# Moving transposes, casts and cluster steps between the first units of a clustered attention and SwiGLU kernel

## The chip, the cores and the metric

The program runs on one core of a Trainium2 chip (trn2). The metric is the device time of one execution in microseconds (us), lower is better; it is quoted as the median of repeated runs. The engines are called as the profile calls them: PE is TensorE's matmul pipe and PEld its weight loads, DVE is VectorE, ACT is ScalarE, POOL is GpSimd, SP is SyncE, which here only starts DMAs.

## The reference

Inputs are q, k and v (4 batches, 8 heads, 768 positions, 64 wide), 16 centroids per head, and the weights of one gated feed-forward layer (512 to 1536 and back to 512).

Each q row and each k row is assigned to the nearest centroid (argmax of the cosine). A q row attends only to the k rows of its own cluster:

```
mask = q_assign[:, :, :, None] == k_assign[:, :, None, :]
scores = where(mask, scale * q @ k.T, -1e9)
attn = softmax(scores);  x = attn @ v        (heads side by side: 3072 rows x 512)
xn = x / sqrt(mean(x*x) + 1e-6) * rms_g
out = (silu(xn @ w_gate) * (xn @ w_val)) @ w_out
```

## The kernel before, in words

**Tiling.** A *unit* is one batch and one half of its 768 query rows, so there are eight units (L47), two for each batch. A unit has 8 heads and each head has three score steps, so 24 *gaps*, counted here from 0 to 23: gap 3h+i is the step (u, h, i) of the code. In each gap `scores` (L298) makes two products of 128 keys by 384 queries on PE, into one of two PSUM buffers, and ACT takes their exponential (L312). In the second gap of a head (i = 1) `pv` (L316) multiplies the probabilities of the head before with its values: 18 matmuls into an accumulator of which there is one, shared by two heads. After the second head of a pair DVE divides by the row sum (L331, L333), and only then can the next pair's first `pv` begin.

**Cluster mask.** q and k are extended from 64 to 80 rows: the 16 rows behind hold a one-hot code of the row's cluster. The one-hot product adds a large constant exactly where the clusters agree, and the exponential's bias takes it off again. There are two ways to make the code. For unit 0's eight heads (groups 0 and 1; a *group* is four heads of a batch) `pair_clusters` (L285) treats two heads at once and `under` (L290) puts the code in place with DVE transposes. For later groups `cluster_steps` (L249) does four heads at once, for q (m = 0) and for k (m = 1): eight small products on PE (L235), a DVE transpose (L238), a maximum (L243), a comparison (L247) and a transpose back (L265); then `place` (L271) writes the code with 16 DMAs that POOL issues, the eight of q first, then the eight of k.

**Preparing a head.** `trans` (L199) transposes q or k on PE in float32 into a PSUM tile (three buffers, the tag "gen", shared with every other small product), and ACT or DVE copies it to `qkT`. `cast` (L213) brings it to bfloat16 in `qext` or `kext`, two casts of 64 x 384 for each of q and k. `vcast` (L222) does v on POOL.

**The order of the work** is written by hand: every engine does its instructions in the order in which the program emits them. Unit 0 has a table `first` (L575) that hangs work behind the gaps; gaps without an entry get `more` (L522), one warm-up matmul that keeps PE busy. `head(n)` (L534) puts k and half of q of head n in place with two `under`; `odd(n)` (L570) puts the other half of q. `late` (L574) are the transposes of group 2, with their copies on DVE. `second_batch` (L527) starts the loads of the second batch on SP, behind a tiny DMA that waits for the last division. Unit 1 runs the table `hooks` and a list of pairs (cost, work) that `attention` (L586) deals out evenly over the gaps: after gap `at` it emits as long as the cost handed out is at most total x (at + 1 - skip) / (gaps - skip). That list holds feed-forward work of unit 0 (`gv`, L376: the gate and value products, with DVE steps L393 and L397), and `prep` (L613): the casts `c` and cluster steps `a` of group 2, then transposes, casts and cluster steps of group 3. In (1, 0, 1) stands `rms(0)` (L353), the normalization of unit 0, and behind it on POOL a copy of one number, `idle` (L615), which waits for the result of `rms(0)`. From unit 2 on, the list starts with the last eight `gv` of the unit before last, then `rms(u - 1)`, the nine parts of the output product `out_mm` (L401, parts of 4 matmuls) mixed with the first transposes `xtrans` (L365), then 16 `gv` mixed with the next group's preparation. Units 2 and 3 use groups 2 and 3: group 3 is needed from gap 12 of unit 2.

**At the start**, five warm-up matmuls (`WARM`, L53) run on a memset piece of `kext[3]` (L110, L111, DVE) before the first transposes; another `busy(1)` stands at L487.

Of the kernel before, what the change touches and what calls it, by code (L numbers as in the profile page):

```python
# [10 lines left out]
BF16 = mybir.dt.bfloat16  # L11
# [11 lines left out]
def kernel(  # L23
# [12 lines left out]
    nc = tc.nc  # L36
    B, H, S, D = q.shape
# [3 lines left out]
    P = 128  # L41
# [3 lines left out]
    HG = 4  # L45
# [4 lines left out]
    FC = DF // P  # L50
    scale = 1.0 / (D ** 0.5)
    KR = D + NC
    WARM = 5  # L53
    CUT = CC + 2 * FC - 8
    LEAD = 7
    NQ, NV = 6, 8
# [3 lines left out]
    const = pool("const", 1)  # L60
# [15 lines left out]
    def src(a, n):  # L76
        b, h = divmod(n, H)
        return a[b, h].rearrange("(p t) d -> p t d", t=ST)
# [6 lines left out]
    def load_qk(n):  # L85
        if n < B * H:
            load(n, 0)
            load(n, 1)

    def load_v(n, vq=None):  # L90
        if n >= B * H:
            return
        stagedv[n] = stage.tile([P, ST, D], F32, tag="vs", name="vs", bufs=NV)
        (vq or nc.sync).dma_start(out=stagedv[n], in_=src(v, n))
# [12 lines left out]

    qext = [const.tile([P, HG, S], BF16, name=f"qext{i}") for i in range(4)]
    kext = [const.tile([P, HG, S], BF16, name=f"kext{i}") for i in range(4)]
    warm = kext[3][:, 0, :512]  # L110
    nc.vector.memset(warm, 1.0)  # L111

    def busy(n, first=True):
        to = ps_a.tile([P, 512], F32, tag="acc", name="warm") if first else \
            ps_g.tile([P, 512], F32, tag="gen", name="warm")
        for i in range(n):
            nc.tensor.matmul(to, lhsT=warm[:, :P], rhs=warm, start=True, stop=True)

    busy(WARM)


    def rsqrt(ms, n):
        half = small.tile([P, HT], I32, tag="half", name="half")[:, :n]
        nc.vector.tensor_scalar(half, ms.bitcast(I32), 1, None, op0=ALU.logical_shift_right)
        yi = small.tile([P, HT], I32, tag="yi", name="yi")[:, :n]
        nc.vector.tensor_scalar(yi, half, -1.0, float(0x5F3759DF), op0=ALU.mult, op1=ALU.add)
        y = yi.bitcast(F32)
        for i in range(3):
            a = small.tile([P, HT], F32, tag="na", name="na")[:, :n]
            nc.vector.scalar_tensor_tensor(a, y, -0.5, y, op0=ALU.mult, op1=ALU.mult)  # L130
            a2 = small.tile([P, HT], F32, tag="nb", name="nb")[:, :n]
            nc.vector.tensor_mul(a2, a, ms)
            y2 = small.tile([P, HT], F32, tag="ny", name="ny")[:, :n]
            nc.vector.scalar_tensor_tensor(y2, a2, 1.5, y, op0=ALU.add, op1=ALU.mult)
            y = y2
        return y
# [76 lines left out]
    def cast(on, g, h, part, es=(0, 1)):  # L213
        for e in es:
            to = (kext if part else qext)[g % 4][:D, h, e * UQ:(e + 1) * UQ]
            of = qkT[g, h // 2][e * D:(e + 1) * D, h % 2, part]
            if on is nc.scalar:
                nc.scalar.copy(to, of)
            else:
                on.tensor_copy(to, of)  # L220

    def vcast(n):  # L222
        nc.gpsimd.tensor_copy(vbf[n // HG % 4][:, n % HG, :, :D], stagedv[n])  # L223
# [117 lines left out]
    def squares(u, t, last):  # L341
        if (t, last) == (0, False):
            sq[u] = small.tile([P, 2, HT], F32, tag="ss", name="ss")
            xn[u] = xp.tile([P, HT, DM], BF16, tag="xn", name="xn")
        c = slice(DM - 2 * D, DM) if last else slice(0, DM - 2 * D)
        to = sq[u][:, int(last), t:t + 1]
        if u == 0:
            nc.vector.scalar_tensor_tensor(xn[u][:, t, c], xs[u][:, t, c], 1.0 / DM, xs[u][:, t, c], op0=ALU.mult,
                                           op1=ALU.mult, accum_out=to)
        else:  # L350
            nc.scalar.activation(xn[u][:, t, c], xs[u][:, t, c], ACT.Square, scale=DM ** -0.5, accum_out=to)

    def rms(u):  # L353
        x, nt = xs[u], UNITS[u][2]
        for t in range(nt):
            squares(u, t, True)
        ms = small.tile([P, HT], F32, tag="ms", name="ms")
        nc.vector.scalar_tensor_tensor(ms[:, :nt], sq[u][:, 0, :nt], 1e-6, sq[u][:, 1, :nt], op0=ALU.add, op1=ALU.add)
        y = rsqrt(ms[:, :nt], nt)
        for t in range(nt):  # L360
            nc.vector.tensor_scalar_mul(xn[u][:, t], x[:, t], y[:, t:t + 1])
# [59 lines left out]
    def group_work(g):  # L421

        t, c = [], []
        for h in range(HG):
            n = g * HG + h
            t += [(0.3, lambda h=h: trans(g, h, 0)), (0.3, lambda h=h: trans(g, h, 1))]

            def casts(h=h, n=n):
                cast(nc.gpsimd, g, h, 0)
                vcast(n)  # L430
                load_qk(n + NQ)
                load_v(n + NV)
                cast(nc.vector, g, h, 1, (0,))
            c += [(0.0, casts), (0.0, lambda h=h: cast(nc.vector, g, h, 1, (1,)))]
        a = []
        for m in range(2):
            a += [(0.0 if i else 0.7, f) for i, f in enumerate(cluster_steps(g, m))]
        a.append((0.0, lambda: [place(nc.gpsimd, g, m) for m in range(2)]))
        return t, c, a
# [5 lines left out]
    def spread(a, b):  # L445

        if not a:
            return list(b)
        w, n = [], 0
        for i, x in enumerate(a):  # L450
            w.append(x)
            while n < len(b) * (i + 1) // len(a):
                w.append(b[n])
                n += 1
        return w

    def ffn_work(u):
        n = UNITS[u][2] / HT
        w = [(0.18 * n, lambda c=c: xtrans(u, c)) for c in range(CC)]
        for f in range(FC):  # L460
            for val in (False, True):
                w.append((0.64 * n, lambda f=f, val=val: gv(u, f, val)))
        return w

    def out_work(u):
        return [(0.86, lambda t=t, p=p: out_mm(u, t, p)) for t in range(UNITS[u][2]) for p in range(3)]

    def border(o, ffn):

        return o[:-3] + ffn[:2] + o[-3:-2] + ffn[2:3] + o[-2:-1] + ffn[3:4] + o[-1:]  # L470
# [6 lines left out]
    def casts(on, n, *what):  # L477
        for m, e in what:
            cast(on, n // HG, n % HG, m, (e,))

    K0, K1, Q0, Q1 = (1, 0), (1, 1), (0, 0), (0, 1)
    pool_ = nc.gpsimd
# [1 line left out]
    trans(0, 0, 0)  # L484
    centroids_t()
    trans(0, 1, 1)
    busy(1)  # L487
    trans(0, 1, 0)
    pair_clusters(0, ps_s.tile([P, UQ], F32, tag="s", name="sc"))
    casts(pool_, 0, K0, Q0, K1)  # L490
# [31 lines left out]
    def more():  # L522
        busy(1, False)
# [3 lines left out]
    def second_batch():  # L527
        nc.sync.dma_start(out=hold, in_=invs[0].rearrange("p a t -> p (a t)"))
        for n in range(H + HG, H + NQ):
            load_qk(n)  # L530
        for n in range(H, H + NV):
            load_v(n)

    def head(n):  # L534
        under(n, 1)
        under(n, 0, 0, 1)
# [33 lines left out]
    def odd(n):  # L570
        under(n, 0, 1, 2)

    early = [lambda h=h, m=m: trans(1, h, m) for h in (2, 3) for m in (1, 0)]
    late = [lambda h=h, m=m: trans(2, h, m, nc.vector) for h in range(HG) for m in (1, 0)]  # L574
    first = {1: gap1, 2: early[0], 3: early[1], 4: lambda: (early[2](), early[3]()), 5: gap5,  # L575
             7: lambda: (more(), head(4)), 8: lambda: (more(), head(5)), 9: gap9,
             10: lambda: (more(), head(6)), 11: lambda: (more(), head(7)),
             14: lambda: (more(), odd(0), second_batch())}
    first.update({15 + i: f for i, f in enumerate(late)})
    first[16] = lambda: (late[1](), odd(1))  # L580
    first[18] = lambda: (late[3](), odd(2))


    due = []
# [22 lines left out]
    for u in range(1, NU):  # L607
        ffn, o, g = ffn_work(u - 1), out_work(u - 2) if u > 1 else [], u + 2
        if u == 1:
            t, c, a = group_work(2)  # L610
            t3, c3, a3 = group_work(3)
            n = 4
            prep = c + a + [x for h in range(HG) for x in t3[max(2 * h, n):2 * h + 2] + c3[2 * h:2 * h + 2]] + a3  # L613
            idle = const.tile([P, 1], BF16)
            hooks = {(1, 0, 1): lambda: (rms(0), nc.gpsimd.tensor_copy(idle, xn[0][:, HT - 1, DM - 1:]))}  # L615
            hooks.update({(1, *divmod(2 + i, HT)): t3[i][1] if i < n else more for i in range(LEAD - 2)})
            hooks.update({(1, h - 1, 0): lambda h=h: odd(h) for h in range(HT, H)})
            attention([(1, h) for h in range(H)], border(o, ffn) + spread(ffn[CC:CUT], prep), LEAD, hooks)
        else:
            fill = ffn_work(u - 2)[CUT:] + [(0.0, lambda u=u: rms(u - 1))] + border(o, ffn)  # L620
            attention([(u, h) for h in range(H)], fill + spread(ffn[CC:CUT], group(g) if g < NG else []), 1)
    pv(NU - 1, H - 1)
    for _, f in ffn_work(NU - 2)[CUT:]:
# [34 lines left out]
```

## Time and profile before

| what | value |
|---|---|
| median of 8 runs | 359.9 us (357.74 to 360.5) |
| the profiled execution's own time | 357.74 us |
| its span in the trace | 355.9 us |
| PE busy | 340.2 us (96%) |
| DVE busy | 232.3 us (65%) |
| ACT busy | 261.7 us (74%) |
| POOL busy | 112.7 us (32%) |
| unit 0: first and last score step | 11.60 and 36.87 us |
| unit 1: first and last score step | 37.42 and 72.25 us |
| unit 2: first and last score step | 73.24 and 113.76 us |
| unit 3: first score step | 114.89 us |

The profiled execution is the fastest of the eight. The spans of the first three units differ because they hold different work: unit 0 has no feed-forward work, unit 1 has two groups to prepare.

How to read the lines: a timeline line gives the start (us), the busy time (us), the engine, the kernel's line, the operation, output <- inputs with the shape, the number of instructions merged, and in brackets how long the engine had sat idle before and whose end released it. In a table by stretches each engine has its busy us and, in parentheses, its number of instructions.

### The profile page before, as it was taken

How to read it: one execution, taken by the hardware profiler on the slowest of the kernel's cores; microseconds unless marked ns; L12 is line 12 of the kernel's file. 1: busy time of each engine (PE TensorE's matmuls, PEld its weight loads, DVE VectorE, ACT ScalarE, POOL GpSimd, SP SyncE). 2: the span in 40 equal slices, each digit the busy share in tenths (PEclk: the TensorE clock that was granted, in tenths of full speed). 3: DMA queues.
4: the chain of work that ended last, by engine and by line, in shares of the span. 5: the costliest groups of instructions: out<-in, count | busy, mean ns of one | idle time of the engine just before them, and what ended most of it. 6: DMA issues, size and time to landing. Idle time of an engine off the chain costs nothing.

```text
span 355.9 us, 7996 instructions
## 1 busy us (share of the span) xinstructions
PE 340.2 (96%) x3028; PEld 207.8 (58%) x3028; DVE 232.3 (65%) x567; ACT 261.7 (74%) x458; POOL 112.7 (32%) x233
## 2 busy tenths in 40 slices
PE   8997898999999999999999999999999999999995
PEld 4545654555675656655575656755566656655552
DVE  4999889986368754786367864687446654674430
ACT  5996966887797868887698877978778877853431
POOL 4999064981133603353041801435000000000000
PEclk9999999999999999999999999999999999999999
DMA  7999997261162013600130001000100011001002
GB/s 268 345 235 212 264 267 246 62 189 40 59 192 80 22 59 104 194 13 14 65 113 2 21 34 61 0 6 20 59 31 0 3 44 47 3 0 67 23 2 89
DMA packets 27158, 31.62 MB, mean 89 GB/s; under 512 B 4464, under 2 KB 24176, under 8 KB 27120
## 3 DMA queue, kind: packets, MB, share of 16 engines
q1 hardware_dynamic: 17808, 24.69, 20.9%
q0 software_dynamic: 8880, 5.91, 9.7%
q8 instruction: 24, 0.39, 0.4%
q10 hardware_dynamic: 432, 0.52, 0.4%
q14 instruction: 14, 0.11, 0.1%
HBM read 28.35 MB, written 6.29 MB: 97 GB/s over the span
## 4 chain that ended last, share of the span: by engine, by line
PE 77%; POOL 7%; ACT 4%; DMA 4%; DVE 4%; issue 2%; SPq 0%; ACTq 0%; POOLq 0%; DVEq 0%
PE o L406 17%; PE val L384 15%; PE gate L384 15%; PE s L308 14%; PE acc L326 8%; PE tq L205 4%; PE sc L235 2%; ACT pT L312 2%; DMA qk<-in_q_dram 2%; POOL qext L220 2%; POOL qext L276 2%; PE tx L371 1%; POOL kext L220 1%; POOL kext L276 1%; POOL vbf L223 1%
## 5 line engine op out<-in xcount | busy, mean ns | idle before, releaser
L312 ACT ACTIVATE pT<-s,off 128x768 bf16<-128x768 f32 x192 | 171.1, 905 | 39.1 <-PE s L308 38.5
L308 PE MATMUL s<-qext,kext 80*128 80x384 bf16 x384 | 93.6, 325 | 3.1 <-ACT pT L312 2.3
L384 PE MATMUL val<-xnT,wv 128*128 128x384 bf16 x384 | 78.1, 326 | 1.8 <-DVE th L393 0.8
L384 PE MATMUL gate<-xnT,wg 128*128 128x384 bf16 x384 | 78.3, 325 | 0.4 <-DVE th L393 0.4
L393 DVE SCALAR_TENSOR_TENSOR th<-th,gate 128x384 f32<-128x384 f32 x84 | 46.3, 552 | 48.7 <-ACT th L392 48.3
L406 PE MATMUL o<-wo,gvT 128*128 128x512 bf16 x288 | 70.5, 379 | 0.4 <-ACT o_sb L417 0.3
L220 POOL CAST qext<-qkT 64x384 bf16<-64x384 f32 x64 | 32.6, 514 | 84.5 <-ACT qkT L211 75.8
L308 PEld LDWEIGHTS <-kext 80*128 80x128 bf16 x384 | 36.9, 98 | 35.2 <-issue 9.1
L392 ACT ACTIVATE th<-gate 128x384 f32<-128x384 f32 x84 | 41.1, 489 | 16.1 <-PE gate L384 15.6
L384 PEld LDWEIGHTS <-wv 128*128 128x128 bf16 x384 | 36.2, 97 | 28.2 <-issue 6.4
L326 PEld LDWEIGHTS <-pT 128*128 128x128 bf16 x1152 | 43.5, 97 | 11.7 <-DVE x L333 2.7
L384 PEld LDWEIGHTS <-wg 128*128 128x128 bf16 x384 | 35.9, 97 | 24.6 <-issue 3.3
L397 DVE SCALAR_TENSOR_TENSOR gvT<-th,val 128x384 bf16<-128x384 f32 x84 | 46.2, 550 | 6.2 <-PE val L384 1.4
L326 PE MATMUL acc<-vbf,pT 128*128 128x65 bf16 x1152 | 45.7, 193 | 2.8 <-POOL vbf L223 2.3
L406 PEld LDWEIGHTS <-gvT 128*128 128x128 bf16 x288 | 26.9, 97 | 26.2 <-issue 0.5
L276 POOL DMA_DIRECT2D qext<-oh x48 | 22.9, 487 | 31.4 <-DVE oh L265 31.4
L205 PE MATMUL tq<-ident_f,qk 128*128 128x128 f32 x192 | 31.1, 281 | 0.6 <-ACT qkT L211 0.3
L211 ACT ACTIVATE qkT<-tq 128x384 f32<-128x384 f32 x56 | 26.3, 498 | 3.2 <-PE tq L205 2.6
L372 DVE TENSOR_SCALAR xnT<-tx,gcol 128x384 bf16<-128x384 bf16 x32 | 12.6, 414 | 23.7 <-PE tx L371 23.6
L417 ACT COPY o_sb<-o 128x512 f32<-128x512 f32 x23 | 13.5, 586 | 19.1 <-PE o L406 18.5
L205 PEld LDWEIGHTS tq<-ident_f,qk 128*128 128x128 f32 x192 | 23.4, 143 | 6.9 <-ACT qkT L211 1.5
L276 POOL DMA_DIRECT2D kext<-oh x48 | 23.1, 488 | 0.9 <-DVE gvT L397 0.9
(71 smaller groups left out, 252.8 us busy)
## 6 DMA issues: line engine op xcount, KB each, us to landing
qk<-in_q_dram SPq DMA_DIRECT2D x32, 192.0 KB, 3.9
vs<-in_v_dram SPq DMA_DIRECT2D x32, 192.0 KB, 4.3
out_dram<-o_sb SPq DMA_DIRECT2D x23, 256.0 KB, 2.0
qk<-in_k_dram SPq DMA_DIRECT2D x30, 192.0 KB, 4.3
wg<-in_moe_w_gate_dram POOLq DMA_DIRECT2D x4, 384.0 KB, 7.1
wv<-in_moe_w_val_dram POOLq DMA_DIRECT2D x4, 384.0 KB, 9.2
wo<-in_moe_w_out_dram POOLq DMA_DIRECT2D x3, 512.0 KB, 16.9
qext<-oh POOLq DMA_DIRECT2D x48, 12.0 KB, 1.6
```

Source lines behind the costliest of these rows:

```text
L205: nc.tensor.transpose(ps[:, i * P:(i + 1) * P], qk[:, part, 2 * i:2 * i + 2].rearrange("p t d -> p (t d)"), ident_f)
L211: nc.scalar.activation(to, ps, ACT.Copy, scale=by)
L220: on.tensor_copy(to, of)
L276: on.dma_start(out=ext[D:D + NC, h, e * UQ:(e + 1) * UQ], in_=put[g, m][32 * h + e * NC:32 * h + (e + 1) * NC])
L308: nc.tensor.matmul(ps[:, j, :w] if nt == HT else flat[:, j * w:(j + 1) * w], lhsT=kext[g % 4][:KR, hh, kc * P:(kc + 1) * P], rhs=qext[g % ...
L312: nc.scalar.activation(pT[u, h][:, n * i:n * i + n, :w], of, ACT.Exp, bias=off, scale=scale * ZS)
L326: nc.tensor.matmul(acc[:, h % 2, t], lhsT=pT[u, h][:, kc, t * P:(t + 1) * P], rhs=vbf[g % 4][:, hh, kc % HT * 2 + kc // HT], start=kc == 0 ...
L384: nc.tensor.matmul(ps, lhsT=w[:, c, f * P:(f + 1) * P], rhs=xnT[u][:, c, :n], start=c == 0, stop=c == CC - 1)
L392: nc.scalar.activation(th, ps, ACT.Tanh, scale=0.5)
L393: nc.vector.scalar_tensor_tensor(th, th, 1.0, ps, op0=ALU.add, op1=ALU.mult)
L397: nc.vector.scalar_tensor_tensor(gvT[u][:, f, :n], gates[u], 0.5, ps, op0=ALU.mult, op1=ALU.mult)
L406: nc.tensor.matmul(outs[u], lhsT=gvT[u][:, f, t * P:(t + 1) * P], rhs=wo[:, f], start=f == 0, stop=f == FC - 1)
```

## The change

Four things are moved, and the start is altered.

1. **Heads 6 and 7.** `head(6)` and `head(7)` go from gaps 10 and 11 of unit 0 to gaps 13 and 14, behind the `pv` of gap 13, whose second half is the division of heads 2 and 3. `odd(0)`, `odd(1)`, `odd(2)` go from gaps 14, 16, 18 to 16, 18, 20.
2. **Group 2's casts.** All 16 casts go to POOL and are emitted in gaps 16, 18, 20 and 22 of unit 0. Before, they stood in unit 1: the eight of q on POOL, the eight of k on DVE. The casts of v and the loads stay in unit 1 (`others`).
3. **Group 3's cluster steps** (`a3`: two times products, maximum, comparison, transpose back, and then `place`) leave unit 1's list and are dealt among the first six output parts of unit 2.
4. **The start.** The warm-up matmuls read a tile of their own, 128 x 128, repeated four times, that POOL memsets, not DVE; there are seven, not five; the single `busy(1)` behind `trans(0, 1, 1)` goes.

```diff
-    WARM = 5
+    WARM = 7
...
-    warm = kext[3][:, 0, :512]
-    nc.vector.memset(warm, 1.0)
+    warm = const.tile([P, P], BF16)
+    nc.gpsimd.memset(warm, 1.0)
...
-            nc.tensor.matmul(to, lhsT=warm[:, :P], rhs=warm, start=True, stop=True)
+            nc.tensor.matmul(to.rearrange("p (a b) -> p a b", b=P), lhsT=warm,
+                             rhs=warm.unsqueeze(1).broadcast_to([P, 4, P]), start=True, stop=True)
...
-            def casts(h=h, n=n):
-                cast(nc.gpsimd, g, h, 0)
+            def others(n=n):
                 vcast(n)
                 load_qk(n + NQ)
                 load_v(n + NV)
+
+            def both(h=h, f=others):
+                cast(nc.gpsimd, g, h, 0)
+                f()
                 cast(nc.vector, g, h, 1, (0,))
-            c += [(0.0, casts), (0.0, lambda h=h: cast(nc.vector, g, h, 1, (1,)))]
+            if g == 2:
+                c.append((0.0, others))
+            else:
+                c += [(0.0, both), (0.0, lambda h=h: cast(nc.vector, g, h, 1, (1,)))]
...
     trans(0, 1, 1)
-    busy(1)
     trans(0, 1, 0)
...
-             10: lambda: (more(), head(6)), 11: lambda: (more(), head(7)),
-             14: lambda: (more(), odd(0), second_batch())}
+             13: lambda: (more(), head(6)), 14: lambda: (more(), head(7), second_batch())}
     first.update({15 + i: f for i, f in enumerate(late)})
-    first[16] = lambda: (late[1](), odd(1))
-    first[18] = lambda: (late[3](), odd(2))
+    for i, n in ((16, 0), (18, 1), (20, 2)):
+        first[i] = lambda i=i, n=n: (late[i - 15](), odd(n))
+    for h in range(HG):
+        first[16 + 2 * h] = lambda h=h, f=first[16 + 2 * h]: (f(), casts(pool_, H + h, K0, Q0, K1, Q1))
...
-            prep = c + a + [x for h in range(HG) for x in t3[max(2 * h, n):2 * h + 2] + c3[2 * h:2 * h + 2]] + a3
+            prep = c + a + [x for h in range(HG) for x in t3[max(2 * h, n):2 * h + 2] + c3[2 * h:2 * h + 2]]
...
-            fill = ffn_work(u - 2)[CUT:] + [(0.0, lambda u=u: rms(u - 1))] + border(o, ffn)
+            fill = ffn_work(u - 2)[CUT:] + [(0.0, lambda u=u: rms(u - 1))]
+            fill += border(spread(o[:-3], a3) + o[-3:], ffn) if u == 2 else border(o, ffn)
```

## The prediction

> **What bounds the kernel now.** I first took the busy time by stretches: unit 0 from its first cluster transpose to its last square, the border up to the first gate product, the rest of unit 1, units 2 and 3.
>
> ```profile
> 8.25:38.57 30.32, 26.12 (x275) 16.80 (x276) 28.86 (x52) 25.45 (x38) 26.25 (x49) 1.00 1.18 264
> 38.57:46.81 8.24, 6.56 (x93) 5.02 (x92) 6.75 (x30) 7.59 (x12) 1.89 (x5) 1.00 1.17 267
> 46.81:73.24 26.43, 24.58 (x231) 13.99 (x231) 24.52 (x53) 19.53 (x32) 18.46 (x37) 1.00 0.68 190
> 73.24:114.89 41.65, 41.44 (x377) 25.73 (x376) 27.16 (x69) 32.88 (x60) 14.59 (x31) 1.00 0.33 107
> 114.89:156.10 41.21, 41.20 (x378) 25.73 (x376) 26.77 (x68) 32.79 (x60) 13.67 (x29) 1.00 0.26 83
> ```
>
> The columns are PE, PEld, DVE, ACT, POOL. From unit 2 on PE is full: 41.20 of 41.21 us. Work put there costs its whole PE time, and a wait of PE there is never won back. Before that DVE is the full engine: 28.86 of 30.32 and 24.52 of 26.43 us; its timeline from 8.25 to 78 us has only two gaps worth the name, 0.85 us at 38.6 and 0.94 us at 47.4. PE's largest loss, in gap 16 of unit 0, I then read in the timeline:
>
> ```profile
> 28.10 0.97 DVE L292 STREAM_TRANSPOSE kext<-pads 32x768 bf16<-32x768 bf16 x1
> ...
> 29.92 0.56 DVE L333 TENSOR_TENSOR x<-acc,inv 128x384 f32<-128x384 f32 x1
> ...
> 30.53 0.60 PEld L326 LDWEIGHTS <-pT 128*128 128x128 bf16 x18 [2.70 <-DVE x L333]
> 30.54 0.72 PE L326 MATMUL acc<-vbf,pT 128*128 128x65 bf16 x18 [2.31 <-POOL vbf L223]
> ```
>
> The value product of head 4 waits 2.31 us for the accumulator, which the division of heads 2, 3 (L333) frees at 30.48. The PE line names POOL, but head 4's values were cast by 25.4; the PEld line names the right one. That division stood behind `head(6)` and `head(7)`, 26.54 to 29.66.
>
> **Part 1, heads 6 and 7.** The comparison ends at 26.43 and head 3's product at 26.21, so the division is now done at 27.2 and gap 16 doesn't wait. But nothing leaves DVE. Behind 26.43 it still has the division (0.8), four `under` (2 x 0.99 + 2 x 0.58), eight copies (0.5 each, start to start), three `odd` (0.59), the division of heads 4, 5 (0.8) and three squares (0.5): 12 us, so it ends at about 38.6 as before. PE meets it again: a transpose needs one of three PSUM buffers, so those of gaps 18 to 22 wait for copies at about 31.0, 31.5, 32.7, 33.2 and 35.1, and head 6's product for the division at 34.6. PE reaches unit 1 some 1.3 us sooner, but the path from there is DVE's: the division of heads 6, 7 starts at 38.75 instead of 39.42, because the 0.85 us gap closes. **-0.67 us.** `head(6)` is ready at 28.8 (needed near 29.6), `head(7)` at 30.4 (near 33.2). `second_batch` follows the division, so SP's loads start 3 us sooner; nothing on the path waits for them.
>
> **Part 2, group 2's casts.** POOL's queue is full up to the output weights, then still:
>
> ```profile
> 34.22 2.22 POOL L194 DMA_DIRECT2D wo<-in_moe_w_out_dram  x3
> 44.80 0.19 POOL L615 COPY idle<-xn 128x1 bf16<-128x1 bf16 x1 [8.36 <-DVE xn L361]
> ```
>
> 16 casts at 0.56 us, start to start, now fill 36.4 to 45.4, all of `rms(0)`'s time (its last instruction ends at 44.65). `idle`, four `vcast` and the value loads queue behind them; nobody waits for those before unit 2. What POOL casts and DVE do to each other, the timeline shows both ways:
>
> ```profile
> 19.39 1.49 POOL L220 CAST kext<-qkT 64x384 bf16<-64x384 f32 x2
> ...
> 19.95 0.56 DVE L247 TENSOR_TENSOR pads<-scT,mx 128x384 bf16<-128x384 f32 x1
> ...
> 48.08 1.07 POOL L220 CAST qext<-qkT 64x384 bf16<-64x384 f32 x2
> ...
> 48.81 1.13 DVE L220 CAST kext<-qkT 64x384 bf16<-64x384 f32 x2
> ...
> 54.09 0.35 DVE L220 CAST kext<-qkT 64x384 bf16<-64x384 f32 x1
> ...
> 71.46 1.28 POOL L220 CAST qext<-qkT 64x384 bf16<-64x384 f32 x2
> 71.59 0.78 DVE L247 TENSOR_TENSOR ohT<-scT,mx 128x384 bf16<-128x384 f32 x1
> ```
>
> A DVE cast takes 0.35 us alone and 0.55 beside POOL's; the comparison 0.56 to 0.78. At 19.95 the comparison kept its 0.56, and POOL's two casts took 1.49 instead of 1.07. So a meeting costs DVE 0.2 us or nothing. On the path of `rms(0)` lie 19 DVE instructions that read two operands from SBUF, as the comparison does, or read and write SBUF alone, as the cast does: six squares, one sum, nine in the loop of the inverse root, three scalings. Ends: 0, and 19 x 0.2 = 3.8, cut to 3.3 because the casts run out near 47. The nearest row, the comparison, went once each way, so I take the half: **+1.6 us.**
>
> [...]
>
> Gain of this part: eight k casts leave DVE in unit 1 (3.3 us there); it is counted next.
>
> **Unit 1 from the first gate product to gap 5 of unit 2** (gaps counted through from here: unit 1 has 24 to 47). DVE loses those 3.3 us and `a3`'s steps (4.5). It keeps 16 `gv` steps (0.5), four `odd` (0.59), two divisions (0.8), eight casts (0.37) and group 2's steps (4.5): 19.5 us. PE has 21.3: gate product 0.65, then 16 gaps of 0.325, 15 `gv` of 0.65, five value products of 0.55, two sets of eight cluster products (0.79), four transposes of 0.33. Dealt out by the list's rule, DVE has 10 us between gaps 35 and 40 where PE has 8.6, runs late, and PE waits 1.4 us for its buffers in gaps 42 to 47. ACT then has three exponentials (0.79), three squares (0.51), a tanh and two copies (0.38) in gaps 45 to 47, 5.0 us against PE's 3.7, and gap 49 waits 1.2. From the gate product to gap 49 that is 21.3 + 1.4 + 0.33 (gap 48) + 1.2 = 24.2 us, before 26.93 (46.81 to 73.74): **-2.7 us.** On to gap 53, 7.7 instead of 7.95: **-0.25 us.** The ends: -5.3 (PE's own work only, no wait) and -1.4 (waits half as long again).
>
> **Part 3, `a3` in unit 2.** Counted from gap 53, counted through, = gap 5 of unit 2 (T, now 81.69):
>
> ```profile
> 81.69 0.49 PE L308 MATMUL s<-qext,kext 80*128 80x384 bf16 x2
> ...
> 84.02 0.16 DVE L358 SCALAR_TENSOR_TENSOR ms<-ss 128x3 f32<-128x3 f32 x1 [1.05 <-ACT xn L351]
> ...
> 86.46 1.28 DVE L361 TENSOR_SCALAR xn<-x,ny 128x512 bf16<-128x512 f32 x3
> ...
> 93.69 0.49 PE L308 MATMUL s<-qext,kext 80*128 80x384 bf16 x2
> ```
>
> `rms(1)` comes first on DVE and ends at T+6.05. Then transpose, maximum, comparison of q (0.6 each), the division of heads 0, 1 (0.8), transpose back: T+9.24. POOL begins 0.29 us later (58.26 to 58.55 for group 2) and issues eight DMAs of q at 0.48; the first of k is issued at T+13.3. From issue to use the chain of waits shows 1.99 us ("75.21 1.99 DMA qext<-oh"), so head 4's scores, gap 12, can start at T+15.35. PE's own work brings it there at T+12.55: now 12.0, plus two cluster sets (1.58), less one output part (0.86) and one `xtrans` (0.17) that the list puts behind gap 12. PE so waits 2.8 us, in gap 11 and before gap 12. Against today: 3.35 up to gap 12 and 1.03 behind it: **+4.4 us.** Of this 2.8 us is the wait; without it 1.6 is left, the moved PE work, which unit 1 has already given back.
>
> **Part 4, the start.** The warm-ups begin near 1.1 us instead of 1.46 and, at 0.427 each, end near 4.1 instead of 3.6. The path runs over the second head's q, used at 6.25, and the single warm-up before it lay in that wait. **0**, between -0.3 and +0.5.
>
> **Sum.** -0.67 + 1.6 - 2.7 - 0.25 + 4.4 = +2.4 us. The profiled execution took 357.74 (span 355.9, the rest around it); it would take 360.1. It is the fastest of eight, 2.2 below their median; on the median 359.9 the forecast is **362.3 us**.
>
> **Rivals.**
> - *The relief is paid in full* (faster). DVE's backlog is gone from `rms(0)` to gap 49, POOL's casts give way and not DVE: 0 instead of 1.6, -5.3 instead of -2.7. Sum -1.8: 358.1. For it: 7.8 of DVE's 27 us leave unit 1. Against: the cast rows, and ACT's burst. It decides once the gain up to gap 49 passes 4.2 us, which is what is left of 4.4 behind it (-0.25); 5.3 make it faster by 0.3%.
> - *Gap 12 doesn't wait*: the codes of k land before PE needs them. +2.4 - 2.8 = -0.4: 359.5, no change. Against: POOL's fixed 0.48 x 8, and q before k in every group.
> [...]
> - That the moves aren't carried out as written can hardly be: each engine runs its queue in order.
>
> **Numbers.** About 0.3% (1.1 us) is what a measurement of this kernel can tell from no change. Forecast 0.45 (own range 360.9 to 363.3), full toll 0.17, gap 12 without wait 0.16, relief in full 0.22. So faster 0.22, within 0.3% 0.18 (the third case and the forecast's edge), slower 0.60. The range reaches from the relief to the full toll, 357.8 to 364.3.
>
> **What would show it.** Right: no idle before gap 16's value product, but idle PE in gaps 18 to 22; L361's first end in unit 1 later than 44.65 and POOL casts across it; PE idle over 2 us before gap 12 of unit 2, released by a DMA of `kext`. Wrong: `rms(0)` at 44.0 with POOL's casts stretched instead; unit 2 without idle; gap 49 (the second of unit 2) before 68.5 us.

## The result, and the profile after

| kernel | median | runs | range |
|---|---|---|---|
| before, beside it | 359.41 us | 32 | 357.4 to 360.91 |
| after | **365.26 us** | 11 | 362.65 to 366.0 |

The medians differ by 5.85 us. The ratio of the runs taken together is 1.0147, with a 95% interval of [1.0125, 1.0168], which is 5.3 us (4.5 to 6.0); the two figures differ because after's runs lie in two groups (last section). The forecast was 362.3 with a range up to 364.3, so the sign was right and the size too small. The profiled execution of after took 366.11 us (span 364.3).

The same table by stretches as for before, with after's own borders (PE, PEld, DVE, ACT, POOL: busy us and instructions; then the granted clock of PE, the DMA share and GB/s):

```profile
8.25:38.57 30.32, 27.50 (x300) 17.90 (x298) 28.84 (x51) 26.74 (x39) 28.21 (x53) 1.00 1.18 278
38.57:49.45 10.88, 6.06 (x71) 4.23 (x70) 10.26 (x31) 6.41 (x11) 8.31 (x18) 0.93 1.20 250
49.45:74.68 25.23, 24.62 (x216) 14.47 (x214) 18.41 (x39) 18.34 (x30) 11.89 (x25) 0.90 0.49 144
74.68:123.32 48.64, 45.15 (x394) 26.20 (x392) 30.68 (x74) 34.20 (x63) 16.37 (x34) 0.96 0.32 101
123.32:164.53 41.21, 41.20 (x378) 25.73 (x376) 26.77 (x68) 32.78 (x60) 13.67 (x29) 1.00 0.26 83
```

Three things are to be seen. DVE is the full engine up to the first gate product, 10.26 of 10.88 us. In unit 1 it has 18.41 us where before had 24.52, as the change meant. And the column of PE's clock, which read 1.00 in every stretch of before, reads 0.93, 0.90 and 0.96 up to unit 3. No term of the prediction held that column. From unit 3 on both kernels need the same 41.21 us.

**Unit 0.** The timeline of after shows that the wait in gap 16 is gone. The division now precedes the `under` of heads 6 and 7, and the value product has no bracket; PE waits for a copy in gap 18 instead:

```profile
26.84 0.56 DVE L334 TENSOR_TENSOR x<-acc,inv 128x384 f32<-128x384 f32 x1
...
27.43 0.97 DVE L293 STREAM_TRANSPOSE kext<-pads 32x768 bf16<-32x768 bf16 x1
...
28.23 0.71 PE L327 MATMUL acc<-vbf,pT 128*128 128x65 bf16 x18
...
31.23 0.55 PE L206 MATMUL tq<-ident_f,qk 128*128 128x128 f32 x3 [0.95 <-DVE qkT L210]
```

(Line numbers of after are one higher than before's here.)

**The border, `rms(0)`.** The timeline from the squares to the first gate products:

```profile
37.23 0.83 DVE L349 SCALAR_TENSOR_TENSOR xn<-x 128x384 bf16<-128x384 f32 x1
...
40.25 0.58 DVE L349 SCALAR_TENSOR_TENSOR xn<-x 128x128 bf16<-128x128 f32 x1
...
41.81 0.43 DVE L125 TENSOR_SCALAR half<-ms 128x3 int32<-128x3 int32 x1
...
43.80 0.42 DVE L135 SCALAR_TENSOR_TENSOR ny<-nb,yi 128x3 f32<-128x3 f32 x1
44.25 0.50 POOL L221 CAST kext<-qkT 64x384 bf16<-64x384 f32 x1
44.25 0.51 DVE L131 SCALAR_TENSOR_TENSOR na<-ny 128x3 f32<-128x3 f32 x1
44.70 0.51 POOL L221 CAST qext<-qkT 64x384 bf16<-64x384 f32 x1
44.80 0.42 DVE L133 TENSOR_TENSOR nb<-na,ms 128x3 f32<-128x3 f32 x1
45.25 0.16 DVE L135 SCALAR_TENSOR_TENSOR ny<-nb,ny 128x3 f32<-128x3 f32 x1
...
46.58 0.23 PE L372 MATMUL tx<-ident,xn 128*128 128x128 bf16 x1 [2.48 <-DVE xn L362]
...
49.12 0.48 PE L372 MATMUL tx<-ident,xn 128*128 128x128 bf16 x3 [1.18 <-DVE xnT L373]
...
49.45 1.44 PE L385 MATMUL gate<-xnT,wg 128*128 128x384 bf16 x4
```

While POOL casts, every small DVE instruction of 128 x 3 numbers takes 0.39 to 0.51 us, each ending within 0.03 us of the end of a cast; the moment the casts stop (45.21), the same instruction takes 0.16. `xn` ends at 47.32, before at 44.65. PE meanwhile idles 4.0 us in gap 31, in four pieces (2.48, 0.17, 0.17 and 1.18). And then the first four gate matmuls take 1.44 us, where before has this:

```profile
46.81 0.97 PE L384 MATMUL gate<-xnT,wg 128*128 128x384 bf16 x4
```

**The clock.** Stretches of 3.41 us of after (PE busy, its instructions, clock, DMA share, GB/s), at the border and in unit 2:

```profile
44.48:47.89 3.41, 0.97 (x9) 1.00 1.21 230
47.89:51.30 3.41, 2.23 (x10) 0.50 1.24 209
51.31:54.72 3.41, 3.41 (x12) 0.50 1.11 344
54.72:58.13 3.41, 3.41 (x40) 1.00 0.93 319
```

```profile
95.68:99.09 3.41, 1.52 (x12) 1.00 0.12 32
99.10:102.51 3.41, 3.41 (x12) 0.50 0.11 34
```

A stretch in which PE was busy for 0.97 or 1.52 of 3.41 us was followed by one or two at **half the granted clock**. Where PE is full there, such a stretch costs an estimated 1.7 us (half of 3.41); `k_codes_by_sync` below shows 1.68.

**Unit 2.** T, gap 53, lies at 83.90. The wait for the codes of k ahead of gap 60 (gap 12 of unit 2) in the timeline:

```profile
93.10 3.81 POOL L277 DMA_DIRECT2D qext<-oh  x8 [16.31 <-DVE oh L266]
...
96.91 3.81 POOL L277 DMA_DIRECT2D kext<-oh  x8
98.52 0.11 PEld L309 LDWEIGHTS <-kext 80*128 80x128 bf16 x2 [2.38 <-DMA kext<-oh]
98.52 0.50 PE L309 MATMUL s<-qext,kext 80*128 80x384 bf16 x2 [1.89 <-DMA kext<-oh]
...
100.67 1.48 PE L385 MATMUL gate<-xnT,wg 128*128 128x384 bf16 x4
```

Where the 8.4 us between the two profiles lie, by the prediction's stretches:

| stretch | before | after | difference | forecast |
|---|---|---|---|---|
| start to first gate product | 46.81 | 49.45 | +2.64 | +0.93 |
| on to gap 49 | 26.93 | 26.85 | -0.08 | -2.7 |
| gap 49 to 53 | 7.95 | 7.60 | -0.35 | -0.25 |
| gap 53 to 60 | 12.00 | 14.62 | +2.62 | +3.35 |
| gap 60 to unit 3 | 21.20 | 24.80 | +3.60 | +1.03 |

The profile of before is one of its luckiest executions. In the 71 executions of before that stood beside the experiments, the mean clock sorts the times: 0.997 or more in 15 (356.99 to 358.05 us), 0.992 to 0.995 in 37 (358.71 to 359.9), 0.989 in 19 (359.88 to 360.82). Profiles with one half-clock stretch ahead of their last 10 us have a mean of 0.993 to 0.995 (`cluster_only`, `start_only`, `casts_behind_rms` below), one with two has 0.991 (`k_codes_by_sync`). So most executions of before seem to lose one or two such stretches too; the profiled one lost none.

### The profile page after: what moved, and what is told of

It reads as the page before. It is cut to its first block, busy times and chain, and to the rows that moved or that the text cites. A ratio compares the mean times of both kernels' runs of the same rounds, so it can differ in the third digit from the quotient of the medians.

```text
span 364.3 us, 7996 instructions
## 1 busy us (share of the span) xinstructions
PE 345.6 (95%) x3029; PEld 210.0 (58%) x3029; DVE 232.8 (64%) x558; ACT 262.0 (72%) x458; POOL 116.3 (32%) x242
## 3 DMA queue, kind: packets, MB, share of 16 engines
q1 hardware_dynamic: 17808, 24.69, 20.2%
## 4 chain that ended last, share of the span: by engine, by line
PE 77%; DVE 11%; ACT 7%; issue 3%; POOL 1%; DMA 1%; ACTq 0%; DVEq 0%; POOLq 0%
PE gate L385 16%; PE val L385 16%; PE o L407 15%; PE s L309 14%; PE acc L327 7%; PE tq L206 4%; ACT pT L313 3%; PE sc L236 3%; PE tx L372 1%; DVE qext L293 1%; PE warm L117 1%; DVE qkT L210 1%; POOL qext L277 1%; ACT qkT L212 1%; ACT xn L352 1%
## 5 line engine op out<-in xcount | busy, mean ns | idle before, releaser
L309 PE MATMUL s<-qext,kext 80*128 80x384 bf16 x384 | 94.7, 329 | 6.0 <-ACT pT L313 3.2
L385 PE MATMUL gate<-xnT,wg 128*128 128x384 bf16 x384 | 80.1, 332 | 0.4 <-DVE gvT L398 0.4
L407 PE MATMUL o<-wo,gvT 128*128 128x512 bf16 x288 | 71.4, 382 | 0.4 <-ACT o_sb L418 0.3
L398 DVE SCALAR_TENSOR_TENSOR gvT<-th,val 128x384 bf16<-128x384 f32 x84 | 46.2, 550 | 8.8 <-PE val L385 4.1
```

Of the source, the lines that this page charges most:

```text
L309: nc.tensor.matmul(ps[:, j, :w] if nt == HT else flat[:, j * w:(j + 1) * w], lhsT=kext[g % 4][:KR, hh, kc * P:(kc + 1) * P], rhs=qext[g % ...
L385: nc.tensor.matmul(ps, lhsT=w[:, c, f * P:(f + 1) * P], rhs=xnT[u][:, c, :n], start=c == 0, stop=c == CC - 1)
L398: nc.vector.scalar_tensor_tensor(gvT[u][:, f, :n], gates[u], 0.5, ps, op0=ALU.mult, op1=ALU.mult)
L407: nc.tensor.matmul(outs[u], lhsT=gvT[u][:, f, t * P:(t + 1) * P], rhs=wo[:, f], start=f == 0, stop=f == FC - 1)
```

## The experiments

**Theory.** The three mechanisms of the prediction are at work (DVE full up to the gate product, its stretched instructions beside POOL's casts, the wait for the codes of k), and a long wait of PE costs more than its length, since the clock is halved behind it (0.50 for 6.83 and 3.41 us in after). **Rivals:** the moved work itself is what costs; or the halved clock comes with the load and has nothing to do with the waits, so that filling them changes nothing.

### The four parts alone

Each is the kernel before with one part of the diff. Part 1, `heads_only`:

```diff
-             10: lambda: (more(), head(6)), 11: lambda: (more(), head(7)),
-             14: lambda: (more(), odd(0), second_batch())}
+             13: lambda: (more(), head(6)), 14: lambda: (more(), head(7), second_batch())}
...
+    for i, n in ((16, 0), (18, 1), (20, 2)):
+        first[i] = lambda i=i, n=n: (late[i - 15](), odd(n))
```

> Only part 1: heads 6, 7 and the three odd() of unit 0 moved. Theory A (VectorE is the full engine of unit 0, so only its 0.85 us of idle time before the division of heads 6, 7 can be won): gap 16 doesn't wait, PE waits in gaps 18 to 22 instead, the whole is 0.7 us faster, 358.7 beside 359.4. Rival B (PE's wait of 2.3 us in gap 16 is worth its length): 357.1.

Measured: 356.52 us, 359.1 for before beside it; ratio 0.9938 [0.9918, 0.9957]. On the median this is the larger gain, the rival's. But the two profiles without a halved clock, before's and this one's, have spans of 355.9 and 355.1: -0.8, close to the -0.67 of the prediction. The 15 executions of before at a clock of 0.997 or more, with a mean of 357.43, and the 12 of this kernel, with a mean of 356.59, give the same -0.8. The division of heads 6 and 7 starts at 38.68 (38.75 was forecast). The rest is the clock: all 12 executions had 0.998 or more, and the wait of gap 16, behind which it reads 0.50 from 29.98 to 33.39 us in the profile of part 4 alone, is gone.

Part 2, `casts_only`:

```diff
+    for h in range(HG):
+        first[16 + 2 * h] = lambda h=h, f=first[16 + 2 * h]: (f(), casts(pool_, H + h, K0, Q0, K1, Q1))
```

with the casts taken out of unit 1's list.

> Only part 2: group 2's 16 casts on GpSimd at the end of unit 0. Theory A (the casts lie over the normalization of unit 0 and hold VectorE up; PE then sits idle long enough that its clock is halved for some us): the normalization's last instruction ends near 47.2 instead of 44.65, granted clock under 1.0 after it, about 3 us slower, 362.4. Rival B (casts and VectorE don't hold each other up on the path; VectorE is relieved by 3.3 us in unit 1): 356.7. Rival C (held up, but the halved clock costs nothing because VectorE paces unit 1): 359.4 + 2.6 - 3.3, near 358.7.

Measured: 360.85 us against 359.1; 1.0056 [1.0035, 1.0076]. The part costs 1.75 us, between the ends that were put to it. In its profile the wait of gap 16 is still there, and 6.83 us behind it are at half clock, so `rms(0)` comes later while POOL casts until 45.0 as in after. Of the small instructions only the first two are stretched (0.38 us at 44.18 and 0.43 at 44.59; from 45.05 on 0.17 and 0.16). In after `rms(0)` begins 2.8 us sooner, in the midst of the casts: without the wait of gap 16, which part 1 takes away, there is no half clock behind it either.

Part 3, `cluster_only`:

```diff
-            prep = c + a + [x for h in range(HG) for x in t3[max(2 * h, n):2 * h + 2] + c3[2 * h:2 * h + 2]] + a3
+            prep = c + a + [x for h in range(HG) for x in t3[max(2 * h, n):2 * h + 2] + c3[2 * h:2 * h + 2]]
...
+            fill += border(spread(o[:-3], a3) + o[-3:], ffn) if u == 2 else border(o, ffn)
```

> Only part 3: group 3's cluster steps at the head of unit 2. Theory A: unit 1 is about 3 us shorter, PE waits about 1.9 us for the codes of k before gap 12 of unit 2 and runs at half clock for 3.4 us behind that: 361.8, or 360.1 if the clock isn't halved. Rival B (no wait there, or it costs nothing): 358.0.

Measured: 362.16 us against 359.1; 1.0113 [1.0065, 1.0161]. The wait stands in its timeline, with the length that it has in after:

```profile
96.12 0.11 PEld L308 LDWEIGHTS <-kext 80*128 80x128 bf16 x2 [2.38 <-DMA kext<-oh]
96.13 0.50 PE L308 MATMUL s<-qext,kext 80*128 80x384 bf16 x2 [1.89 <-DMA kext<-oh]
```

In this profile the clock stays full in unit 2 (the wait fell into a stretch with 1.71 us of busy PE), so the part is seen by itself: from gap 49 to unit 3 it takes 45.34 us (73.90 to 119.24), before 41.15 (73.74 to 114.89), so +4.19. The prediction had -0.25 + 4.4 = +4.15. Unit 1 from gap 31 to 49 gives back 1.7 (27.80 against 29.49).

Part 4, `start_only`:

```diff
-    WARM = 5
+    WARM = 7
...
-    busy(1)
     trans(0, 1, 0)
```

and the warm-ups' own tile, set by POOL.

> Only part 4: seven warm-up matmuls on a tile that GpSimd sets, no single one behind. Theory A: the first scores come at 11.77 instead of 11.60 as in the changed kernel, 0.2 us slower, 359.6. Rival B (earlier warm-up, earlier full clock): 0.3 us faster, 359.1.

Measured: 358.55 us against 359.1; 0.9969 [0.9944, 0.9993], hardly more than nothing, and part of it may be the clock: 5 of its 12 executions had 0.997 or more and none 0.989, of before 15 and 19 of 71. Part 1 with it, `heads_start`:

> Before with parts 1 and 4 only, heads 6 and 7 behind the division and the altered start. Theory (the gain of each is real and they lie on different stretches: -2.6 with the clock drop of gap 16, -0.5 at the start; but the start's gain was partly luck of the clock): 355.7 to 356.6, no drop in the clock between 8 us and the end. Rival (DVE is the bound of unit 0 from its start, so a start that reaches it sooner is given back): no better than heads alone, 356.5 or more.

Measured: 357.03 us against 359.44; 0.9932 [0.9908, 0.9956], no better than part 1 alone (0.9938), as the rival said: nothing of an earlier start is left.

The four ratios multiply to 1.0075, and all parts together cost 1.0147; the gap of 0.007 is little more than the intervals of the four taken together (some 0.006 each way). The profiles say that the parts aren't independent: with part 1 the casts stretch the instructions of `rms(0)` by twice as much (1.7 us in `casts_only`, 3.4 in after), and behind PE's longer wait in gap 31 after has two half-clock stretches, where `casts_only` has one.

### Taking the costs out of after

**The casts behind the result of `rms(0)`,** `casts_behind_rms`: the same 16 casts on POOL, emitted where `idle` waits for `xn`.

```diff
-        first[16 + 2 * h] = lambda h=h, f=first[16 + 2 * h]: (f(), casts(pool_, H + h, K0, Q0, K1, Q1))
...
-            hooks = {(1, 0, 1): lambda: (rms(0), nc.gpsimd.tensor_copy(idle, xn[0][:, HT - 1, DM - 1:]))}
+            hooks = {(1, 0, 1): lambda: (rms(0), nc.gpsimd.tensor_copy(idle, xn[0][:, HT - 1, DM - 1:]),
+                                         [casts(pool_, H + h, K0, Q0, K1, Q1) for h in range(HG)])}
```

> The changed kernel with the same 16 casts on GpSimd, but emitted behind the copy that waits for the normalization of unit 0. Theory A (the casts hold up VectorE's normalization, and only there): the normalization's last instruction ends near 43.9 instead of 47.3, no halved clock in unit 1, 360 instead of 365.3. Rival B (VectorE is held up wherever the casts lie): no better than 363.5. Rival C (the cost is group 3's codes alone, and the longer normalization is hidden): 365.

Measured: 358.97 us against 359.42; 0.9991 [0.9967, 1.0015]; 6.3 below after. Its timeline:

```profile
39.27 0.28 DVE L349 SCALAR_TENSOR_TENSOR xn<-x 128x128 bf16<-128x128 f32 x1
...
39.80 0.17 DVE L125 TENSOR_SCALAR half<-ms 128x3 int32<-128x3 int32 x1
40.00 0.17 DVE L127 TENSOR_SCALAR yi<-half 128x3 int32<-128x3 int32 x1
40.21 0.16 DVE L131 SCALAR_TENSOR_TENSOR na<-yi 128x3 f32<-128x3 f32 x1
...
43.52 0.50 POOL L221 CAST kext<-qkT 64x384 bf16<-64x384 f32 x1
```

Every stretched instruction is short again. From the end of the division of heads 6 and 7 to the end of `xn` it is 4.44 us (38.81 to 43.25), in after 7.32 (40.00 to 47.32): 2.88, and two squares ahead of the division took 0.83 instead of 0.56 us, 0.54 more. So the casts cost DVE **3.4 us** on the path in this pair. It isn't the same in every execution: `gap31_warm` has 3.5, while in the profiles of `k_codes_by_sync` and `warm_in_waits` the two squares keep their 0.55 us and the rest takes 7.42 and 7.25, so that the casts cost 3.0 and 2.8. With the half-clock stretches behind gap 31, which are gone since PE waits less there (2.4 us, below), that makes 5.8 of the 6.3. From the gate product to gap 49 it is now 24.45 us (45.37 to 69.82), and the prediction had 24.2.

**The codes of k by another queue,** `k_codes_by_sync`: SP issues group 3's eight DMAs of k beside POOL's eight of q.

```diff
-        a.append((0.0, lambda: [place(nc.gpsimd, g, m) for m in range(2)]))
+        a.append((0.0, lambda: [place(nc.sync if g == 3 and m else nc.gpsimd, g, m) for m in range(2)]))
```

> The changed kernel, but the eight codes of k of group 3 are written by DMAs from SyncE's queue, beside GpSimd's eight of q, not behind them. Theory A (head 4's scores wait for eight DMAs issued before the first of k): no wait before gap 12 of unit 2 and no halved clock behind it, 3.6 us less: 361.7. Rival B (SyncE's queue, with an output store before them, brings them as late): 365.3.

Measured: 362.17 us against 359.42; 1.0080 [1.0044, 1.0115]; 3.1 below after. Its timeline shows SP starting before POOL is done with q, and a wait of 0.26 us instead of 1.89:

```profile
92.63 3.83 POOL L277 DMA_DIRECT2D qext<-oh  x8 [16.31 <-DVE oh L266]
...
94.62 4.99 SPq L277 DMA_DIRECT2D kext<-oh  x8
...
96.42 0.50 PE L309 MATMUL s<-qext,kext 80*128 80x384 bf16 x2 [0.26 <-DMA kext<-oh]
```

The half-clock stretch in unit 2 went with the wait: from gap 60 to unit 3 it is 23.12 us, in after 24.80. So 1.63 of wait and 1.68 of clock, 3.3 in all, beside 3.1 between the medians.

**The waits kept, but filled,** `gap31_warm` and `warm_in_waits`: warm-up matmuls whose result nobody reads, in PE's queue where it waits; they add work and bring nothing forward that PE waits for.

```diff
+            hooks[1, 2, 1] = lambda: busy(11, False)
```

and, in the second kernel alone, ahead of gap 60:

```diff
+                      {(2, 3, 2): lambda: busy(7, False)} if u == 2 else {})
```

> The changed kernel with 11 warm-up matmuls in gap 31 (unit 1) and 7 in gap 11 of unit 2, where TensorE waits in any case; nothing that it waits for comes sooner. Theory A (a wait costs more than its length, because the clock is halved behind it): granted clock 1.00 throughout, the waits end when they did, 3.5 us less: 361.8. Rival B (the halved clock is hidden by VectorE and ScalarE): 365.3 or a little more.

> The changed kernel with 11 warm-up matmuls in gap 31 alone, where PE waits for rms(0); the wait in gap 11 of unit 2 is left as it is. Nothing that PE waits for comes sooner. Theory (a wait of PE also costs the halved clock behind it): the drop of 6.83 us behind gap 31 goes and the one of 3.41 behind gap 60 stays; -2.3 to -2.9 of the 4.2 that both fillings gave, 362.4 to 363.0. Rival (the fillings gave their gain elsewhere, or the clock falls anyway by the load): 364.5 or more.

Measured: both filled 361.06 us, 1.0053 [1.0032, 1.0075], 4.2 below after, with a clock of 0.998 or more in eight of ten executions (0.993 and 0.994 in the others); gap 31 alone 361.85 us, 1.0078 [1.0050, 1.0106], 3.4 below after, somewhat more than expected: in its profile the wait before gap 60 (1.89 us, as in after) found no half-clock stretch behind it. In the timeline of `gap31_warm`:

```profile
43.18 2.54 PE L117 MATMUL warm<-warm 128*128 128x512 bf16 x11
45.89 0.23 PE L372 MATMUL tx<-ident,xn 128*128 128x128 bf16 x1 [0.17 <-DVE xn L362]
...
48.42 0.33 PE L372 MATMUL tx<-ident,xn 128*128 128x128 bf16 x3 [1.18 <-DVE xnT L373]
48.75 0.97 PE L385 MATMUL gate<-xnT,wg 128*128 128x384 bf16 x4
```

`xn` comes as late as in after (6.6 us from the end of the division to PE's transpose in both: 39.30 to 45.89, 40.00 to 46.58), but the gate product runs at full speed, its four matmuls in 0.97 us where after took 1.44. From that transpose to gap 49 it is 27.29 us (to 73.18), in after 29.72 (to 76.30): **2.4 us** are the price of the halved clock behind gap 31 by itself. The rival that the clock falls by the load is refuted.

**The same in before,** `gap16_filled`: nine warm-up matmuls ahead of gap 16's wait, and the two heads left where they were.

```diff
+    first[15] = lambda: (late[0](), busy(9, False))
```

> The kernel before with 9 warm-up matmuls in front of gap 16 of unit 0, in its wait of 2.3 us. Theory A (in most executions of the kernel before, though not in the one first profiled, that wait halves the clock too): 1.7 us faster than the kernel before, 357.5. Rival B (the wait costs its length and no more): 359.2, no change.

Measured: 357.89 us against 359.42; 0.9964 [0.9943, 0.9984]. All 12 executions had a clock of 0.997 or more and lie between 357.23 and 358.1. So 1.5 us of before's median were the clock behind its own wait. That the wait of 2.31 us itself was not on the path, as the prediction said, is shown by part 1 alone, which took it away and won 0.8 us where the clock is full.

### Both mended, and the best version

`both_mended` is after with the casts behind `rms(0)` and the codes of k by SP.

> The changed kernel with its 16 casts emitted behind the result of rms(0) and with group 3's k codes placed by SP. Each mend alone took 6.3 us and 3.1 us off (358.97 and 362.17 against 365.26). Theory (wait plus halved clock behind each wait): no wait of PE over 1.9 us is left between gap 17 of unit 0 and unit 3, so the clock stays full in unit 2, and the time is that of the casts-behind version less its gap-12 wait of 1.91 and less its clock drop of 3.41 at half speed (1.7): 358.97 - 1.9 - 1.7 = 355.4, up to 356.5 where some idle stays in gap 63. Rival (the moved PE work of group 3's cluster steps in unit 2, about 1.6 us, can't be won back, and the two mends overlap): 357.5 to 359.

Measured: 356.85 us against 359.44; 0.9931 [0.9907, 0.9956], a little over what the theory said: from gap 60 to unit 3 23.12 us are needed and not 22.2, of which 0.48 are idle PE in gap 63, most of it a wait for DVE's `gvT` (L398).

`mended_a3_in_unit1` is after with the casts behind `rms(0)`, and part 3 undone (`+ a3` back in unit 1's list).

> The changed kernel with its casts behind the result of rms(0) and with group 3's cluster steps back in unit 1's list, so part 3 undone. Theory (part 3 costs its PE work, its wait and the clock behind the wait): gap 12 of unit 2 doesn't wait, and against the casts-behind version (358.97) 1.6 + 1.9 + 1.7 go from unit 2 while unit 1 grows by what the steps cost there, 1.6 of PE or up to 3.3 if DVE is again its bound: 355.4 to 357. Rival (DVE in unit 1 can't carry the steps beside the casts, and the delay of a whole 4.5 us of DVE work comes back in unit 1): 358.5 to 360.

Measured: **354.5 us** (354.3 to 354.82) against 359.44; 0.9865 [0.9839, 0.9891], below what both theories said. In its timeline gap 60 has no wait left, and the gate product behind it takes 0.81 us:

```profile
89.53 1.02 PE L407 MATMUL o<-wo,gvT 128*128 128x512 bf16 x4
90.39 0.49 PE L309 MATMUL s<-qext,kext 80*128 80x384 bf16 x2
90.72 0.81 PE L385 MATMUL gate<-xnT,wg 128*128 128x384 bf16 x4
```

Its stretches, from the first gate product to unit 2 and unit 2 itself:

```profile
45.59:70.28 24.69, 23.82 (x231) 13.82 (x230) 21.94 (x46) 19.19 (x32) 22.12 (x46) 1.00 0.86 216
70.28:111.59 41.31, 41.18 (x376) 25.73 (x376) 26.87 (x68) 32.85 (x60) 14.16 (x30) 1.00 0.31 98
```

The cluster steps cost unit 1 0.74 us (gate product to gap 49: 25.19 us, 24.45 with them moved), and unit 2 is full again, 41.18 of 41.31. DVE has room for them in unit 1 once the casts are POOL's: 21.94 of 24.69 us, before 24.52 of 26.43. Part 2 gave the room in unit 1, and part 3 took the steps out of it, to unit 2, where PE has none.

## Why the prediction was right and wrong

- **Part 1, -0.67: right.** -0.8 where the clock is full. What it missed is that removing a wait of 2.31 us also removes the halved clock behind it, 1.5 us on before's median.
- **Part 2, "the nearest row, the comparison, went once each way, so I take the half: +1.6 us": the first failed step.** The casts cost 3.4 us on the path in after's profile (2.8 to 3.5 in the four profiles that have them there), the upper end, which the prediction put at 3.3 and calls the full toll in its chances. One row gave a toll per meeting of 0.2 us; measured it is up to 0.35 (0.51 for 0.16): each of the eight short instructions from 41.39 to 45.22 us ended within 0.03 us of the end of a cast. Also the two integer steps with one input (L125, L127: 0.43 and 0.51 for 0.17) were stretched, which the count of 19 left out. Twelve instructions met the casts, and their excess adds up to 3.4. One comparison that kept its 0.56 us was no reason for the half.
- **Gate product to gap 49, -2.7: right, and hidden.** 24.45 us with the casts out of the way, 24.2 forecast. In after its first 5.27 us (49.45 to 54.72) ran at half clock with PE busy throughout, which took nearly all of it away again.
- **Part 3, +4.4 with a wait of 2.8 us: right in sum, not in its pieces.** 4.19 against 4.15 in the profile where the clock is full. The wait is 1.89, for the first DMA of k lands 1.57 us after its issue and not 1.99, and POOL begins 0.3 sooner; behind gap 60 the moved work costs 1.9 us (23.12 against 21.20), not 1.03, and 0.48 of it are idle PE in gap 63.
- **Part 4, 0: right** within what can be measured: the first score step comes at 11.44 us in the mean of nine profiles with the new start (11.11 to 11.77), at 11.60 in five with the old (11.14 to 11.98).
- **The sum: the second failed step, and the larger one.** It priced each wait of PE at its length and the clock at nothing, without a reason. The clock was read as 1.00 in all stretches of before and so entered no term. Behind the 4.0 us idle of gap 31 it fell for 6.83 us, behind gap 60's 1.89 for 3.41: filling both waits took 4.2 us off (2.4 and 1.7 by the profiles).
- **The base.** Against the profile, the forecast was +2.4, and the two profiles differ by 8.4. Against the medians it is 5.85, as most executions of before, by their clocks, hold half-clock stretches that its profile doesn't. The prediction saw that its profile lay 2.2 us below the median and added the difference without asking for its cause. Without such stretches it is 361.06 (after, both waits filled) against 357.89 (before, gap 16 filled): +3.2, or 0.8 above the forecast. The other 2.7 are what the clock takes from after (4.2) less what it takes from before (1.5). The terms at their measured sizes (-0.8, 3.4, -2.5, 4.2) make 4.3, 1.1 more than these 3.2; 0.6 of that is the casts, which cost 2.8 and not 3.4 in the profile with both waits filled, and where the rest lies no run shows.

Of the signs that the prediction named for being right, two came as said (no idle before gap 16's value product; `xn` late with casts across it) and two came smaller: PE idles in gap 18, but not in gaps 19 to 22, and it is released by a DMA of `kext` ahead of gap 60 after 1.89 us, not over 2.

## What to carry to other kernels

A wait of PE with full work behind it cost its length here, and could cost the halved clock of the next microseconds too (1.7 us behind gap 60, 2.4 behind gap 31): waits of 1.89 and 2.31 us did so in some executions and not in others. Price both, and where a wait can't be removed, fill it with matmuls. Before the forecast is set on one profile, put its time beside the other runs' times and clocks, for it may be the one without a halved stretch. Work moved to an idle engine isn't free if the short instructions on the path take longer beside it: here 16 casts of 0.5 us held up a dozen small DVE instructions, and with the first cast 7 us later, behind them, nothing waited.

## What the runs showed of the hardware

**The clock changed on a grid.** In after it changes at 47.89, 54.72, 99.09 and 102.50 us: distances of 6.83, 44.37 and 3.41, which are 2, 13 and 1 times 3.413. The first record of a full clock starts at 6.93 us in after, 12 times 3.413 ahead of the first change, and at 5.30 in before, so each has a phase of its own. The profiles of part 4 alone and of `casts_behind_rms` have one half-clock stretch of that length each (29.98 to 33.39 and 92.52 to 95.93 us).

**Halved periods followed periods with little busy time.** The 14 profiles have eight drops of the clock ahead of their last 10 us, and for six of them the rows give the full-clock period of 3.41 us ahead: PE was busy in it for 0.97 and 1.52 us (after), 1.44 (part 4 alone), 1.50 (`casts_behind_rms`), 1.55 and 2.00 (`casts_only`). Eight full-clock periods with 1.71 to 2.63 us had a full clock behind them (1.71 in `cluster_only`, 2.03 in `gap31_warm`, 2.23 and 2.31 in after, 2.02, 2.07, 2.37 and 2.63 in before). The profile of part 4 alone and that of before, the same wait of gap 16 in both, with another phase:

```profile
26.57:29.98 3.41, 1.44 (x9) 1.00 1.31 199
29.98:33.39 3.41, 2.98 (x27) 0.50 1.22 208
```

```profile
25.78:29.19 3.41, 2.37 (x25) 1.00 1.30 195
29.20:32.61 3.41, 2.07 (x30) 1.00 1.32 210
```

Before's wait was shared between two periods, and neither had a halved clock behind it. The exception among the six is the second one of `casts_only`, with 2.00 us busy and a halved clock behind it:

```profile
46.83:50.24 3.41, 2.00 (x32) 1.00 1.16 260
50.25:53.65 3.40, 3.40 (x14) 0.50 1.18 270
```

In the last 10 us, which the count leaves out, it doesn't hold either: two periods with 1.53 and 1.54 us of busy PE (after, from 358.50; before, from 350.05) were followed by a full-clock one. So the busy time of one period, as the profile models it, doesn't settle what comes behind it, and what does stays open. A wait of 1.89 us had a halved clock behind it where it lay within one period (after), and none in `cluster_only`, where 1.70 us of the same wait fell into one period and the rest into the next.

**The phase seems to make a kernel's times fall in groups.** After's runs lie at 362.65 to 363.08 us (clock 0.988 or 0.989) and at 365.11 to 366.0 (0.986, one 0.978), and before's in the three groups above. The kernels whose waits are gone or filled lie close together: `mended_a3_in_unit1` within 0.52 us, all its runs at 0.997 or more, and `gap16_filled` within 0.9. That a group is set by where the waits fall on the grid is shown by single profiles; the runs without a trace show only their mean clock, which fits.
